# Loading K in one piece and scoring it by key head, in a one-token attention and MLP kernel

## Chip, cores and metric

The kernel runs on one core of a Trainium2 chip. The metric is the device time of one execution in microseconds (us). The kernel before takes 98.69 us, the median of three runs (98.69 to 98.81). All figures beside it come from one execution that the hardware profiler recorded.

## The reference

One token with 1024 features is normalised; the result `xn` goes through an attention block and an MLP block, and both are added to the input.

```python
def _A_ref(x, k_cache, v_cache, wq, wo):
    B, Sq, D = x.shape                                 # 1, 1, 1024
    Hq, Dh = 32, 128
    Hkv, Sk = k_cache.shape[1], k_cache.shape[2]       # 4 key heads, 65536 keys
    W = min(4096, max(256, Sk // 4))                   # the last 4096 keys
    rep = Hq // Hkv                                    # 8 query heads share a key head
    q = (x @ wq).reshape(B, Sq, Hq, Dh) ...
    k = jnp.repeat(k_cache[:, :, Sk - W:, :], rep, axis=1)
    v = jnp.repeat(v_cache[:, :, Sk - W:, :], rep, axis=1)
    scores = jnp.einsum("bhqd,bhkd->bhqk", q, k) * (Dh ** -0.5)
    p = _softmax(scores, axis=-1)
    o = jnp.einsum("bhqk,bhkd->bhqd", p, v)
    return (...).reshape(B, Sq, Hq * Dh) @ wo

def _B_ref(x, w1, b1, w2, b2):                         # F = 3584
    y = _layernorm(x, axis=-1)
    h = _gelu(jnp.einsum("bsd,df->bsf", y, w1) + b1)
    return jnp.einsum("bsf,fd->bsd", h, w2) + b2

xn = _layernorm(x, axis=-1)
return x + _A_ref(xn, ...) + _B_ref(xn, ...)
```

All weights and caches are bf16. Per execution the kernel reads wq (8.4 MB), the last 4096 keys of K for four heads (4.2 MB), W1 (7.3 MB), the same of V (4.2 MB), W2 (7.3 MB) and wo (8.4 MB), each once.

## The kernel before

The kernel is written out by hand: every engine has its own list of instructions, and semaphores tie the lists together. There is no scheduler; the order in the text is the order on each engine.

**SP's queue** issues all large loads, in this order: wq in two pieces, K in two pieces (`load_k(0)`, `load_k(1)`, L228 and L229), W1, and then, each behind a wait, V (L303, after the last transpose of K, since V is written over K in `KV`), W2 in two pieces (L305, after the last scores, since W2 is written over wq in `BIG`), and wo in four pieces (L308, after the hidden layer, over W1). The transfers go through one queue in that order.

**K.** `load_k(c)` brings two of the four key heads at a time. Their 4096 keys are cut into 64 runs; a partition of `KV` gets one run of one head, 64 keys of 128 features or 16 KB, so the 128 partitions are 64 runs times two heads. VectorE then transposes `KV` into `KT` in four pieces (`turn_k`, L277, four transposes of 128 x 4096 bf16, handled as 2048 words of 32 bits), in blocks of 32 partitions by 32 words. After that the partitions of `KT` carry features and its columns carry keys: neighbouring words of a row belong to alternating heads, and the two halves of a word are two neighbouring features.

**Queries.** TensorE multiplies the normalised token with wq into bank 7 (L427, eight turns of eight matmuls), ScalarE copies the result out (`Q32`, L286), VectorE transposes it (`QTB`, L288), and VectorE and ScalarE place it into `QBD`, which is zero elsewhere, in four copies (L299, L301).

**Scores.** `OTHER` and `ALT` are constants made by GpSimd at the start. Four matmuls (L434) write −1e30 into those places of banks 3 to 6 where a query head would meet the keys of the other head of the pair, and zero elsewhere; each is followed by two matmuls on zeros (`busy`) that keep TensorE running. Then 32 matmuls of 512 columns (L452 to L461) add the scores: over two pairs, two halves, two banks, two halves of a word (`w`) and two halves of the features (`j`). The moving operand is `K4`, and with it neighbouring columns of a matmul are neighbouring words of `KT`, 4 bytes apart:

```python
K4 = KT[:, :].rearrange("p (x k w) -> p x w k", k=64, w=2)
...
K4[:, bass.ds(c * 64 + i * 32 + 16 * n, 16), w, 32 * j:32 * j + 32]
```

**Softmax.** VectorE takes the maximum over the four banks in two pieces (L324), gathers the quarters of the partitions (L328, L330) and writes the negative scaled maximum, with −1e30 in the rows of the other pair (`MASKC`), into `NMB` (L333). ScalarE takes exp of all 2048 columns twice (L338), once for each pair, with row sums into `SUMP`; it writes each pair's two of four neighbouring columns of `P`. VectorE transposes `P` into `PT` (L343).

**The rest, in TensorE's order.** After the scores TensorE waits for W1 (L467) and computes the hidden layer (seven turns of eight matmuls); it then adds the row sums (L474), turns the hidden layer into columns (L477), multiplies `PT` with V (L483, eight turns of four matmuls, needs `PT` and V), and runs eleven rounds of eight matmuls (L489) over the 28 row blocks of W2 and the first 16 of wo. Each round waits on `s_feed`, which GpSimd raises as W2 and wo land. The last 16 row blocks of wo go through narrow matmuls (L504), and the result is copied out and stored.

Of the kernel before, what the change touches and what calls it, by code (L numbers as in the profile page):

```python
# [5 lines left out]
ALU = mybir.AluOpType  # L6
ACTF = mybir.ActivationFunctionType
AX = mybir.AxisListType
# [6 lines left out]
REP = HQ // HKV  # L15
SK = 65536
W = 4096
# [10 lines left out]
PAIRS = 2  # L28
FAR = -1e30
QW = 512 + 32  # L30
# [24 lines left out]
def bass_parallel_sum__sliding_block_cached__mixer_channel_mlp__decode_kernel(  # L55
# [13 lines left out]
    SCALE = float(DH) ** -0.5  # L69
# [15 lines left out]
    DVE = Track(nc, "S_DVE")  # L85
    ACT = Track(nc, "S_ACT")
    POOL = Track(nc, "S_POOL")
# [14 lines left out]
    MASKC = sb("MASKC", [32, PAIRS], f32)  # L102
    OTHER = sb("OTHER", [2, 128], bf16)
    ALT = sb("ALT", [2, 512], bf16)
# [4 lines left out]
    BN = sb("BN", [128, 24], f32)  # L109
# [6 lines left out]
    QBD = sb("QBD", [128, PAIRS * QW], bf16)  # L116
# [5 lines left out]
    NMB = sb("NMB", [128, PAIRS], f32)  # L122
# [5 lines left out]
    SUMP = sb("SUMP", [128, PAIRS], f32)  # L128
    TOT = sb("TOT", [128, 1], f32)
# [9 lines left out]
    P, PT = KT[:, 0:4096], KT[:, 4096:8192]  # L139
# [16 lines left out]
    C = {}  # L156
# [14 lines left out]
    def pool_wait():  # L171
# [5 lines left out]
    C["QBD"] = POOL.mark(pool.memset(QBD[:, :], 0.0))  # L177
# [9 lines left out]
    POOL.mark(pool.memset(OTHER[:, :], FAR))  # L187
    POOL.mark(pool.memset(ALT[:, :], 0.0))
# [12 lines left out]
    POOL.mark(pool.affine_select(  # L201
        out=OTHER[:, :].rearrange("p (x g h) -> p x g h", g=2, h=REP),
        in_=OTHER[:, :].rearrange("p (x g h) -> p x g h", g=2, h=REP),
        pattern=[[0, 8], [-1, 2], [0, REP]], compare_op=ALU.not_equal, fill=0.0, base=0, channel_multiplier=1))
    POOL.mark(pool.affine_select(
        out=ALT[:, :].rearrange("p (x g) -> p x g", g=2), in_=ALT[:, :].rearrange("p (x g) -> p x g", g=2),
        pattern=[[0, 256], [-1, 2]], compare_op=ALU.not_equal, fill=1.0, base=0, channel_multiplier=1))
    for c in range(PAIRS):
        POOL.mark(pool.affine_select(  # L209
            out=MASKC[:, c:c + 1], in_=YZ[0:32, 0:1], pattern=[[0, 1]], compare_op=ALU.is_ge, fill=FAR,  # L210
            base=-16 if c else 15, channel_multiplier=1 if c else -1))
# [9 lines left out]
    def pairs(cache, c):  # L221
        return cache[0, 2 * c:2 * c + 2, SK - W:SK, :].rearrange("g (m i) d -> m g (i d)", m=64)
# [54 lines left out]
    def turn_k(n):  # L277
        dve.wait_ge(s_k[n // 2], 16)
# [13 lines left out]
    QD = QBD[:, :].rearrange("p (c x) -> p c x", c=PAIRS)[:, :, 0:512].rearrange("p c (w n e) -> p w c n e", w=2, e=2)  # L292
    QS = QTB.rearrange("p (j e c w) -> p w c j e", j=4, e=2, w=2)
    for b in range(4):
        rows = slice(32 * b, 32 * b + 32)
        to = QD[rows, :, :, 32 * b:32 * b + 16, :].rearrange("p w c (u j) e -> p w c u j e", j=4)
        of = QS[rows, :, 0:4 * PAIRS, :, :].rearrange("p w (c u) j e -> p w c u j e", c=PAIRS)
# [5 lines left out]
    sp.dma_start(V, A_v_cache[0, :, SK - W:SK, :].rearrange("g (m i) d -> m g (i d)", m=32)).then_inc(s_v, 16)  # L303
    sp.wait_ge(done["sc"], 4)
# [16 lines left out]
    S = PS[:, 3 * 512:7 * 512]  # L321
    for n in range(2):
        dve.wait_ge(done["sc"], 3 + n)
        C["mx"] = DVE.mark(dve.tensor_reduce(  # L324
            out=MX2[:, n:n + 1], in_=S[:, 1024 * n:1024 * n + 1024], axis=AX.X, op=ALU.max))
# [6 lines left out]
    for b in range(4):  # L332
        C["nmb"] = DVE.mark(dve.scalar_tensor_tensor(  # L333
            out=NMB[32 * b:32 * b + 32, :], in0=MXR[:, :].to_broadcast([32, PAIRS]), scalar=-SCALE, in1=MASKC[:, :],
            op0=ALU.mult, op1=ALU.add))
    act.wait_ge(DVE.sem, C["nmb"])
    for c in range(PAIRS):
# [30 lines left out]
    DVE.mark(dve.tensor_reduce(  # L368
        out=TOT[:, :], in_=PS[:, 3 * 512:3 * 512 + PAIRS], axis=AX.X, op=ALU.add))
    dve_wait()  # L370
    DVE.mark(dve.reciprocal(out=REC[:, :], in_=TOT[:, :]))
    dve_wait()
# [43 lines left out]
    def add(to, lhsT, rhs, **place):  # L416
        return pe.matmul(to, lhsT=lhsT, rhs=rhs, start=False, stop=False, skip_group_check=True, **place)  # L417
# [15 lines left out]
    with pe.Fori(0, 4) as n:  # L433
        pe.matmul(PS[:, bass.ds(n * 512 + 3 * 512, 512)], lhsT=OTHER[:, :], rhs=ALT[:, :], start=True, stop=False,  # L434
                  skip_group_check=True)
        busy(GO, bank(1), start=False, stop=False)
# [13 lines left out]
    pe.wait_ge(DVE.sem, C["d_QBD"])  # L450
# [23 lines left out]
    pe.matmul(PS[:, 3 * 512:3 * 512 + PAIRS], lhsT=B128[:, :], rhs=SUMP[:, :]).then_inc(done["tot"], 1)  # L474
# [77 lines left out]
```

## Time and profile before

| What | Value |
|---|---|
| Median of three runs | 98.69 us (98.69 to 98.81) |
| The profiled execution | 98.65 us |
| Its span in the profile | 97.2 us |
| Bytes moved | 39.88 MB, mean 410 GB/s over the span |
| TensorE busy, matmuls | 80.1 us (82% of the span), 389 matmuls |
| VectorE, ScalarE, GpSimd busy | 33.3, 13.0 and 9.7 us |
| Granted TensorE clock | full in every slice |

The span is the time between the first and last instruction that the profiler saw; the device time holds some 1.4 us more. A busy share is an average over the whole span and says little about which wait ends last. What decides is the chain of waits, which is followed back from the last instruction, and the idle time in front of each group on its engine with what ended it. Times "from the start" below count from the start of the span. PE stands for TensorE, PEld for its weight loads, DVE for VectorE, ACT for ScalarE, POOL for GpSimd, SP for SyncE; a "q" behind a name means its sequencer or its issuing of transfers.

The stretches between the landings of the loads look like this (start and end in us, busy time of TensorE's matmuls, share of DMA, rate):

| Stretch | Landing at its end | TensorE busy | DMA share | GB/s |
|---|---|---|---|---|
| 22.40 to 32.20 | K | 9.63 | 1.13 | 479 |
| 32.20 to 49.10 | W1 | 15.47 | 0.95 | 411 |
| 49.10 to 58.80 | V | 9.29 | 1.00 | 432 |
| 58.80 to 75.80 | W2 | 15.74 | 1.00 | 432 |
| 75.80 to 95.20 | wo | 17.43 | 0.95 | 406 |

A packet counts in the stretch in which it begins, which is why a share can pass 1 and its neighbour stay under it.

### The profile page before, as it was taken

The numbers are of one execution on the slowest core, as the hardware profiler recorded it, in microseconds if no ns is written. First come the engines' busy times: TensorE is split into PE (matmuls) and PEld (weight loads), VectorE is DVE, ScalarE is ACT, GpSimd is POOL, SyncE is SP. The second block draws the span as 40 slices with busy tenths as digits, with TensorE's granted clock in tenths as the row PEclk, the third lists the DMA queues.
The fourth block names the chain that finished last, engine by engine and source line by source line (L and its number), as shares of the span: only waits on it lengthen the run. The fifth ranks groups of instructions, "written<-read, shape, count | busy, mean of one in ns | idle before, by whom it ended". The sixth has DMA issues, their size and how long they took to land.

```text
span 97.2 us, 1407 instructions
## 1 busy us (share of the span) xinstructions
PE 80.1 (82%) x389; PEld 33.8 (35%) x400; DVE 33.3 (34%) x54; ACT 13.0 (13%) x20; POOL 9.7 (10%) x25
## 2 busy tenths in 40 slices
PE   0000999997999999999669999799999999779982
PEld 0000233443444432344134444433343443334451
DVE  0000589860069995000760593050049100000001
ACT  0880000050000005000019400200000100000001
POOL 6999300000000000000000000000000000000000
PEclk9999999999999999999999999999999999999999
DMA  2998888899999988888999999999899999889890
GB/s 64 650 473 377 377 377 377 377 452 425 414 418 516 637 377 377 377 377 377 499 431 445 431 431 445 431 431 394 374 485 485 445 445 445 381 374 445 377 384 2
DMA packets 1845, 39.88 MB, mean 410 GB/s; under 512 B 306, under 2 KB 308, under 8 KB 564
## 3 DMA queue, kind: packets, MB, share of 16 engines
q1 hardware_dynamic: 1732, 39.85, 95.6%
q10 hardware_dynamic: 112, 0.01, 0.1%
q8 instruction: 1, 0.02, 0.1%
HBM read 39.86 MB, written 0.00 MB: 410 GB/s over the span
## 4 chain that ended last, share of the span: by engine, by line
DMA 80%; PE 14%; SPq 3%; issue 1%; DVE 0%
DMA BIG<-in_B_w_dram 47%; DMA BIG<-in_A_wo_dram 33%; PE PS L417 14%; SPq L225 1%; SPq L160 1%; SPq L310 1%; DVE Pb L395 0%; PE PS L499 0%
## 5 line engine op out<-in xcount | busy, mean ns | idle before, releaser
L417 PE MATMUL PS<-BIG,GO 128*128 (+1 forms) x137 | 21.5, 334 | 2.2 <-POOLq L408 1.2
L417 PEld LDWEIGHTS PS<-BIG,GO 128*128 (+1 forms) x148 | 9.9, 97 | 13.9 <-issue 5.9
L417 PE MATMUL PS<-BIG,XZ 128*128 x64 | 14.0, 379 | 0.6 <-DMA BIG<-in_A_wq_dram 0.6
L417 PE MATMUL PS<-BIG,YZ 128*128 x56 | 12.4, 379 | 1.8 <-DMA BIG<-in_B_w_dram 1.8
L279 DVE STREAM_TRANSPOSE KT<-KV 128x2048 f32<-128x2048 f32 x4 | 9.0, 2290 | 6.8 <-DMA KV<-in_A_k_cache_dram 6.8
L421 PE MATMUL PS<-QBD 128*128 128x512 bf16 x38 | 11.2, 467 | 0.1
L417 PEld LDWEIGHTS PS<-BIG,XZ 128*128 x64 | 6.2, 98 | 8.3 <-issue 2.0
L413 PE MATMUL PS<-XBRP,onesb 1*128 1x512 bf16 x2 | 1.0, 605 | 9.7 <-DMA XBRP<-in_A_x_dram 9.7
L417 PE MATMUL PS<-KV,KT 128*128 x32 | 8.3, 381 | 0.5
L417 PEld LDWEIGHTS PS<-BIG,YZ 128*128 x56 | 5.4, 96 | 8.9 <-issue 3.0
L395 DVE CAST Pb<-PS 64x256 bf16<-64x256 f32 x1 | 0.4, 417 | 19.9 <-PE PS L499 19.9
L417 PE MATMUL PS<-KT,QBD 128*128 x32 | 7.1, 378 | 0.0
L421 PEld LDWEIGHTS PS<-QBD 128*128 128x128 bf16 x38 | 4.3, 115 | 7.4 <-issue 4.8
L343 DVE STREAM_TRANSPOSE KT<-KT 128x4096 bf16<-128x4096 bf16 x1 | 4.4, 4446 | 4.1 <-ACT KT L338 4.1
L338 ACT ACTIVATE KT<-PS,NMB 128x2048 bf16<-128x2048 f32 x2 | 3.9, 1963 | 12.1 <-DVE NMB L333 12.1
L324 DVE TENSOR_REDUCE MX<-PS 128x1 f32<-128x1024 f32 x2 | 2.5, 1225 | 8.2 <-PE PS L417 8.2
L237 DVE BATCH_NORM_STATS2 BN<-PS 128x6 f32<-128x512 f32 x2 | 1.3, 689 | 10.7 <-PE PS L413 10.7
L417 PEld LDWEIGHTS PS<-KV,KT 128*128 x32 | 3.1, 96 | 5.3 <-issue 3.8
L417 PEld LDWEIGHTS PS<-KT,QBD 128*128 x32 | 3.0, 97 | 4.0 <-issue 0.4
L375 DVE TENSOR_SCALAR QBD<-PS,REC 32x128 f32<-32x128 f32 x4 | 1.4, 345 | 6.9 <-PE PS L417 6.8
L413 PEld LDWEIGHTS PS<-XBRP,onesb 1*128 1x128 bf16 x2 | 0.1, 98 | 9.6 <-POOL MASKC L209 9.6
L395 ACT ACTIVATE Pb<-PS 64x256 bf16<-64x256 f32 x1 | 0.4, 381 | 19.5 <-PE PS L499 19.5
(78 smaller groups left out, 42.0 us busy)
## 6 DMA issues: line engine op xcount, KB each, us to landing
BIG<-in_A_wq_dram SPq DMA_DIRECT2D x1, 7168.0 KB, 21.1
BIG<-in_B_w_dram SPq DMA_DIRECT2D x1, 7168.0 KB, 46.1
KV<-in_A_k_cache_dram SPq DMA_DIRECT2D x2, 2048.0 KB, 27.8
KV<-in_A_v_cache_dram SPq DMA_DIRECT2D x1, 4096.0 KB, 22.1
BIG<-in_B_w_dram SPq DMA_DIRECT2D x1, 4096.0 KB, 20.8
BIG<-in_A_wo_dram SPq DMA_DIRECT2D x1, 4096.0 KB, 23.5
BIG<-in_B_w_dram SPq DMA_DIRECT2D x1, 3072.0 KB, 27.7
BIG<-in_A_wo_dram SPq DMA_DIRECT2D x1, 3072.0 KB, 30.4
```

Of the source, the lines that this page charges most:

```text
L160: sp.dma_start(dst[:, c0 * width:(c0 + n) * width].rearrange("p (c n) -> p c n", c=n), src[:, c0:c0 + n, :],).then_inc(semaphores[j], 16)
L225: sp.dma_start(KV[:, c * 8192:(c + 1) * 8192], pairs(A_k_cache, c)).then_inc(s_k[c], 16)
L237: DVE.mark(dve.bn_stats(out=BN[:, 12 * n + 6 * i:12 * n + 6 * i + 6], in_=src[:, 512 * i:512 * i + 512]))
L279: C["kt", n] = DVE.mark(dve.transpose(KT[:, n * 4096:(n + 1) * 4096].bitcast(f32), KV[:, n * 4096:(n + 1) * 4096].bitcast(f32)))
L310: sp.dma_start(BIG[:, first:first + n * D], wo_flat[:, c0 * D:(c0 + n) * D]).then_inc(s_wo[j] if j else s_feed, HALF_FEED)
L324: C["mx"] = DVE.mark(dve.tensor_reduce(out=MX2[:, n:n + 1], in_=S[:, 1024 * n:1024 * n + 1024], axis=AX.X, op=ALU.max))
L338: C["exp"] = ACT.mark(act.activation(out=P.rearrange("p (r x g) -> p r x g", r=2, g=4)[:, :, :, 2 * c:2 * c + 2], in_=S.rearrange("p (x r ...
L343: C["d_pt"] = DVE.mark(dve.transpose(PT, P))
L375: DVE.mark(dve.tensor_scalar(out=ONM[:, 128 * j:128 * j + 128], in0=PS[32 * j:32 * j + 32, 512 + 128 * j:512 + 128 * j + 128], scalar1=REC ...
L413: last = pe.matmul(bank(2 + i), lhsT=onesb[0:1, :], rhs=XB[0:1, 8 * i:8 * i + 8, :])
L417: return pe.matmul(to, lhsT=lhsT, rhs=rhs, start=False, stop=False, skip_group_check=True, **place)
L421: pe.matmul(to, lhsT=zeros[:, 0:128], rhs=zeros[:, 0:512], skip_group_check=True, **how)
```

## The change

All four key heads of K come in one load, in the layout that V already has: 32 runs of 128 keys for each head, 32 KB per partition, the partitions being 32 runs times four heads. After the transposes the words of four heads alternate in `KT`, and the scores pick one head at a time: eight columns of a head lie four words, 16 bytes, apart. No head meets another head's keys, so nothing is masked, the scores fill two banks instead of four, and one exp over 1024 columns takes the place of two over 2048. `P` has to be zero where a row's head doesn't own the column, so VectorE multiplies the exp, repeated four times, with a table `OWN` of ones and zeros (128 x 4).

In the order of the engines: the masking matmuls become matmuls on zeros of the same size; the score loop runs over two halves and four heads with four matmuls to a turn; the third and fourth transpose of K come after the copies into `QBD`; V's load waits for the fourth, as before. The constants `OTHER`, `ALT` and `MASKC` are gone, `QBD` is about twice as wide and is cleared in two pieces. `BN` gets a wider allocation of which the same columns are used.

```diff
-    s_k = sems("s_k", PAIRS)
+    s_k = nc.alloc_semaphore("s_k")
...
+    OWN = sb("OWN", [128, GROUPS], bf16)
...
-    BN = sb("BN", [128, 24], f32)
+    BN = sb("BN", [128, 96], f32)
...
-    QBD = sb("QBD", [128, PAIRS * QW], bf16)
+    QBD = sb("QBD", [128, GROUPS * QW], bf16)
...
-    P, PT = KT[:, 0:4096], KT[:, 4096:8192]
+    P, PT, PX = KT[:, 0:4096], KT[:, 4096:8192], KT[:, 8192:9216]
...
-    C["QBD"] = POOL.mark(pool.memset(QBD[:, :], 0.0))
+    C["QBD"] = POOL.mark(pool.memset(QBD[:, 0:1024], 0.0))
...
-    POOL.mark(pool.memset(OTHER[:, :], FAR))
-    POOL.mark(pool.memset(ALT[:, :], 0.0))
+    POOL.mark(pool.memset(QBD[:, 1024:], 0.0))
...
-    def load_k(c):
-        sp.dma_start(KV[:, c * 8192:(c + 1) * 8192], pairs(A_k_cache, c)).then_inc(s_k[c], 16)
+    def by_group(cache):
+        return cache[0, :, SK - W:SK, :].rearrange("g (m i) d -> m g (i d)", m=32)
...
-    load_k(0)
-    load_k(1)
+    sp.dma_start(KV[:, :], by_group(A_k_cache)).then_inc(s_k, 16)
...
-    for n in range(4):
+        DVE.mark(dve.tensor_reduce(
+            out=OWN[:, :], in_=identb[:, :].rearrange("p (b g h) -> p g b h", b=4, g=GROUPS), axis=AX.XY, op=ALU.add))
+
+    dve.wait_ge(s_k, 16)
+    for n in range(2):
         turn_k(n)
...
             C["a_QBD"] = ACT.mark(act.activation(out=to, in_=of, func=ACTF.Copy))
+    for n in range(2, 4):
+        turn_k(n)
     sp.wait_ge(DVE.sem, C["kt", 3])
...
-    sp.wait_ge(done["sc"], 4)
+    sp.wait_ge(done["sc"], 2 * GROUPS)
...
-    S = PS[:, 3 * 512:7 * 512]
+    S = PS[:, 3 * 512:5 * 512]
...
-    for c in range(PAIRS):
-        C["exp"] = ACT.mark(act.activation(
-            out=P.rearrange("p (r x g) -> p r x g", r=2, g=4)[:, :, :, 2 * c:2 * c + 2],
-            in_=S.rearrange("p (x r g) -> p r x g", r=2, g=2),
-            func=ACTF.Exp, bias=NMB[:, c:c + 1], scale=SCALE, accum_out=SUMP[:, c:c + 1]))
+    C["exp"] = ACT.mark(act.activation(
+        out=PX, in_=S, func=ACTF.Exp, bias=NMB[:, :], scale=SCALE, accum_out=SUMP[:, :]))
     dve.wait_ge(ACT.sem, C["exp"])
+    DVE.mark(dve.tensor_tensor(
+        out=P.rearrange("p (x g) -> p x g", g=GROUPS), in0=PX.unsqueeze(2).to_broadcast([128, 1024, GROUPS]),
+        in1=OWN[:, :].unsqueeze(1).to_broadcast([128, 1024, GROUPS]), op=ALU.mult))
+    dve_wait()
     C["d_pt"] = DVE.mark(dve.transpose(PT, P))
...
-    K4 = KT[:, :].rearrange("p (x k w) -> p x w k", k=64, w=2)
-    with pe.Fori(0, PAIRS) as c:
+    pe.reg_mov(turn, C["d_QBD"])
+    K4 = KT[:, :].rearrange("p (x j k g w) -> p x j g w k", j=2, k=REP, g=GROUPS, w=2)
+    with pe.Fori(0, 2) as i:
         pe.wait_ge(ACT.sem, C["a_QBD"])
-        with pe.Fori(0, 2) as i:
-            for n in range(2):
-                for w in range(2):
-                    for j in range(2):
-                        last = add(PS[:, bass.ds(i * 1024 + (3 + n) * 512, 512)],
-                                   QBD[:, bass.ds(c * 512 + (w * 256 + j), 128, step=2)],
-                                   K4[:, bass.ds(c * 64 + i * 32 + 16 * n, 16), w, 32 * j:32 * j + 32])
+        pe.wait_ge(DVE.sem, turn)
+        pe.reg_add(turn, turn, C["kt", 3] - C["d_QBD"])
+        with pe.Fori(0, GROUPS) as g:
+            for w in range(2):
+                for j in range(2):
+                    last = add(PS[:, bass.ds(i * 512 + 3 * 512, 512)],
+                               QBD[:, bass.ds(g * 512 + (w * 256 + j), 128, step=2)],
+                               K4[:, bass.ds(i * 64, 64), j, bass.ds(g, 1), w, :])
             last.then_inc(done["sc"], 1)
```

More of the change, by code (lines that the diff above doesn't have):

```diff
@@ L27 @@
 XW = 136
-PAIRS = 2
-FAR = -1e30
-QW = 512 + 32
+GROUPS = 4
+QW = 512 + 16
 XP = 72
@@ L121, in bass_parallel_sum__sliding_block_cached__mixer_channel_mlp__decode_kernel @@
     MXR = sb("MXR", [32, 1], f32)
-    NMB = sb("NMB", [128, PAIRS], f32)
+    NMB = sb("NMB", [128, 1], f32)
     Pb = sb("Pb", [128, 2048], bf16)
@@ L127, in bass_parallel_sum__sliding_block_cached__mixer_channel_mlp__decode_kernel @@
     QTB = Pb[:, 512:1024]
-    SUMP = sb("SUMP", [128, PAIRS], f32)
-    TOT = sb("TOT", [128, 1], f32)
+    SUMP = sb("SUMP", [128, 1], f32)
     REC = sb("REC", [128, 1], f32)
@@ L277, in turn_k @@
     def turn_k(n):
-        dve.wait_ge(s_k[n // 2], 16)
         C["kt", n] = DVE.mark(dve.transpose(
             KT[:, n * 4096:(n + 1) * 4096].bitcast(f32), KV[:, n * 4096:(n + 1) * 4096].bitcast(f32)))
-    for n in range(4):
+    with nc.allow_low_precision(reason="sums of a one and zeros"):
+        DVE.mark(dve.tensor_reduce(
+            out=OWN[:, :], in_=identb[:, :].rearrange("p (b g h) -> p g b h", b=4, g=GROUPS), axis=AX.XY, op=ALU.add))
+    dve.wait_ge(s_k, 16)
+    for n in range(2):
         turn_k(n)
@@ L332, in bass_parallel_sum__sliding_block_cached__mixer_channel_mlp__decode_kernel @@
     for b in range(4):
[L333 to L335 removed]
+        C["nmb"] = DVE.mark(dve.tensor_scalar(
+            out=NMB[32 * b:32 * b + 32, :], in0=MXR[:, :], scalar1=-SCALE, scalar2=None, op0=ALU.mult))
     act.wait_ge(DVE.sem, C["nmb"])
[L337 to L341 removed]
+    C["exp"] = ACT.mark(act.activation(
+        out=PX, in_=S, func=ACTF.Exp, bias=NMB[:, :], scale=SCALE, accum_out=SUMP[:, :]))
     dve.wait_ge(ACT.sem, C["exp"])
+    DVE.mark(dve.tensor_tensor(
+        out=P.rearrange("p (x g) -> p x g", g=GROUPS), in0=PX.unsqueeze(2).to_broadcast([128, 1024, GROUPS]),
+        in1=OWN[:, :].unsqueeze(1).to_broadcast([128, 1024, GROUPS]), op=ALU.mult))
+    dve_wait()
     C["d_pt"] = DVE.mark(dve.transpose(PT, P))
@@ L367, in bass_parallel_sum__sliding_block_cached__mixer_channel_mlp__decode_kernel @@
     dve.wait_ge(done["tot"], 1)
[L368 to L371, printed above, removed]
+    DVE.mark(dve.reciprocal(out=REC[:, :], in_=PS[:, 3 * 512:3 * 512 + 1]))
     dve_wait()
@@ L433, in bass_parallel_sum__sliding_block_cached__mixer_channel_mlp__decode_kernel @@
     with pe.Fori(0, 4) as n:
-        pe.matmul(PS[:, bass.ds(n * 512 + 3 * 512, 512)], lhsT=OTHER[:, :], rhs=ALT[:, :], start=True, stop=False,
+        pe.matmul(PS[:, bass.ds(n * 512 + 3 * 512, 512)], lhsT=GO[:, 0:128], rhs=GO[:, 0:512], start=True, stop=False,
                   skip_group_check=True)
@@ L473, in bass_parallel_sum__sliding_block_cached__mixer_channel_mlp__decode_kernel @@
     pe.wait_ge(ACT.sem, C["exp"])
-    pe.matmul(PS[:, 3 * 512:3 * 512 + PAIRS], lhsT=B128[:, :], rhs=SUMP[:, :]).then_inc(done["tot"], 1)
+    pe.matmul(PS[:, 3 * 512:3 * 512 + 1], lhsT=B128[:, :], rhs=SUMP[:, :]).then_inc(done["tot"], 1)
     pe.wait_ge(ACT.sem, C["a_h8"])
```

28 lines of the change are left out of this document (6 added, 22 removed).

## The prediction

> **What bounds the kernel now.** I read the chain of waits first, then the DMA page, then the timeline of TensorE, then the groups by shape.
>
> ```profile
> DMA 80%; PE 14%; SPq 3%; issue 1%; DVE 0%
> ...
> q1 hardware_dynamic: 1732, 39.85, 95.6%
> ```
>
> Chain and queues: the end hangs on DMA, and SP's queue keeps all 16 engines 95.6% busy over the span. 39.85 MB pass through one queue in the order wq, K, K, W1, V, W2, W2, wo. Time goes only if fewer microseconds of transfer remain, and is lost if the queue runs dry or TensorE falls behind the last transfers. So the cover of TensorE is what has to be read:
>
> ```profile
> 36.75 0.54 SPq L303 DMA_DIRECT2D KV<-in_A_v_cache_dram  x1
> 47.70 0.83 SPq L160 DMA_DIRECT2D BIG<-in_B_w_dram  x2
> 61.98 1.76 SPq L310 DMA_DIRECT2D BIG<-in_A_wo_dram  x4
> ```
> ```profile
> 40.56 7.11 PE L417 MATMUL PS<-KT,QBD 128*128 x32
> 49.51 12.44 PE L417 MATMUL PS<-BIG,YZ 128*128 x56 [1.84 <-DMA BIG<-in_B_w_dram]
> ...
> 62.95 8.73 PE L417 MATMUL PS<-KV,KT 128*128 x32
> 71.77 12.79 PE L417 MATMUL PS<-BIG,GO 128*128 x49
> 85.75 8.56 PE L417 MATMUL PS<-BIG,GO 128*128 x68 [1.19 <-POOLq L408]
> 94.61 0.73 PE L417 MATMUL PS<-BIG,GO 128*32 128x256 bf16 x20 [0.31 <-DMA BIG<-in_A_wo_dram]
> ```
>
> First column is the start, second the length, in us. TensorE runs scores, hidden layer, P·V, W2 and wo rounds in one line, and waits for data three times from the scores on: 1.84 us before the hidden layer, 1.19 before the first wo round, 0.31 before the last rows. So the scores may end 1.84 us later for nothing, and the hidden layer may start 1.19 + 0.31 = 1.50 us later before the end moves. From 40.56 to 49.51 + 1.50 = 51.0 there are 10.45 us for 32 score matmuls: 0.326 us each, against (7.11 − 0.38) / 31 = 0.217 now.
>
> **K in one load.** Two loads of 16 KB rows take from wq's landing (1.26 + 21.1 = 22.4) to the transposes' release at 32.2: 9.8 us. V, the same bytes in 32 KB rows, takes from W1's landing (3.04 + 46.1 = 49.1) to its own (36.75 + 22.1 = 58.85): 9.7 us. Gain 0.1 us (0.05 to 0.2 by the rounding), and one issue of some 0.6 us less on SP at a time when nothing waits for SP.
>
> The first two transposes lose their early start (27.52): all K lands at 32.1. Two of them (4.5 us) end at 36.6, before the copy of q frees VectorE at 37.2, so that costs nothing. The other two now stand behind the q transpose and the QBD copies (0.45 + 0.57, ending at 38.3) and end at 42.8. The second half of the scores needs them at 40.56 + 3.5 = 44.0 at the earliest: hidden by the first half. V's issue moves from 36.75 to 42.8; W1 covers it until 49.1.
>
> **Set-up.** POOL loses five constants (0.2 + 0.5 + 0.4 + 2.3 + 0.3) and gains about 1.0 for the other half of QBD; TensorE starts with x at 9.67 anyway. VectorE gains the reduction for OWN, at most the 1.03 us of the 128x512 reduction at L272, in its 6.6 us of idling for K. QBD copies have as many elements as before, the zeroing matmuls as many columns as the masking ones.
>
> **From scores to P.** The last maximum starts at 47.70 and exp at 50.64: 2.9 us, less 0.55 for half the columns (1225 ns for 1024) = 2.4. One exp of 1024 columns: half of 1963 plus 0.2 for its sum, 1.2 to 1.3, for two (3.9 + 0.4). New is the spread, 4096 elements on VectorE between exp and transpose. The nearest row, L256, multiplies 1024 bf16 by a repeated operand in 1225 ns: four times that is 4.9 us; the transpose of 4096 bf16 takes 4.45. I take 4.5. With the transpose: 2.4 + 1.25 + 4.5 + 4.45 = 12.6 us after the scores. P·V starts 12.44 + 1.0 after the hidden layer starts, so with the hidden layer right behind the scores the cover is 0.8 us, 0.4 at 4.9. Without cover each microsecond of it would delay P·V by one.
>
> **The scores.** Still 32 matmuls of 512 columns, now in eight turns of four. P·V has that form and takes 8.73 us, so 7.1 to 8.7 by the rows: at 8.7 they end at 49.3, inside the 1.84.
>
> The open price is the read of K. Before, a matmul reads columns 4 bytes apart (one bf16 of each pair); now the eight of a head lie 16 bytes apart, each column a piece by itself. No row of TensorE reads that. Lower end: no price, 0.217. The rows that bound it:
>
> ```profile
> L260 DVE TENSOR_REDUCE XNT<-Pb 128x8 f32<-128x1024 bf16 x1 | 2.0, 1986 | 0.0
> L324 DVE TENSOR_REDUCE MX<-PS 128x1 f32<-128x1024 f32 x2 | 2.5, 1225 | 8.2 <-PE PS L417 8.2
> L417 PEld LDWEIGHTS PS<-FLIP,H 8*128 8x128 bf16 x4 | 0.2, 113 | 0.6 <-ACT H L345 0.6
> L440 PEld LDWEIGHTS PS<-B1R,E 32*128 32x128 bf16 x4 | 0.2, 92 | 0.4 <-issue 0.4
> ```
>
> After the bar: busy us, mean ns of one. L260 sums 1024 bf16 read 16 bytes apart, exactly the new step: 1986 ns, where a reduction over as many adjacent elements takes 1225. With some 150 ns fixed (a reduction of 8 elements, L330, takes 149) that is 1.79 ns an element against 1.05. TensorE's weight load of H8 in steps of 8 bytes takes 113 ns, one of adjacent columns 92: a step costs there too, though only 0.16 ns a column. TensorE's own bound: the W1 matmuls read pieces of four columns (8 bytes) 56 bytes apart at full rate, 0.423 ns a column, so a separate piece costs it no more than 4 × 0.423 = 1.69 ns. With one column to a piece that is at most 512 × 1.69 = 866 ns a matmul.
>
> The ends are far apart: 0.217 us (hidden; by the weight loads' 0.16 ns, 0.30, hidden too) and 0.866. I take 0.866: L260 reads with this very step, at 1.79 ns, and a fetch of about 1.7 ns for each piece fits the reduction, and leaves W1 at full rate as the trace has it.
>
> [...]
>
> **Sum.** 32 × 0.866 = 27.7: the scores end at 68.3, the hidden layer starts there, 18.8 us later than 49.51; P (68.3 + 12.6 = 80.9) is ready before P·V (62.95 + 18.8 = 81.7). The waits of 1.19 and 0.31 vanish: the end moves by 18.8 − 1.5 = 17.3. The profiled execution took 98.65 (span 97.2, 1.4 around it), 0.04 under the median of 98.69: 98.65 + 17.3 = 115.9.
>
> Behind SP's wait for the scores stand W2's two loads and then wo. W2 is issued at 68.7 instead of 47.70; V is through at 58.7, and the first issue of the run (0.80) shows transfers about 1 us later, so DMA stands still for some 11 us. All of wo is in at 95.2 + 11 = 106, TensorE's last round is later (85.75 + 18.8 − 1.2 = 103.3 for its start, and 10 more), so TensorE sets the end.
>
> **Rivals.**
> - *Half rate.* 0.433 us a matmul: scores end at 54.4, the hidden layer 4.9 late, end +3.4: **102.1**. W2 is issued at 54.8, in time before V's end. For it: a step costs VectorE a factor of 1.7, not 4; TensorE may fetch a piece in less than the 1.69 that its rows allow. Against: VectorE's 1.79 ns for one piece.
> - *The step costs TensorE nothing that shows* (not slower). Place: the K read. Price up to 0.326 us a matmul. The scores stay under the loads of W1 and V, and the 0.1 us of K remains: 98.65 − 0.1 = **98.55**. It holds as long as 32 scores end by 51.0, and tips beyond. For it: full rate at 4 bytes and at W1's pieces, weight loads that lose only a fifth. Against: L260. If the one load gains nothing either, 98.65.
> - *The spread is late.* At L260's 1.79 ns it would take 7.3 us, 2.8 over, 2 us past its cover; TensorE's 1.5 us of waits take most: **99.2**, with free scores. Against: L256 repeats an operand in the same way at 1.2 ns.
>
> **Chances.** Full price per piece 0.43 (own range 112.5 to 117.5: a piece at 1.5 to 1.79 ns), half rate 0.22, hidden 0.30, spread late 0.05. A difference of 0.2% (0.2 us) is about what a measurement of this kernel can tell from none. Of the hidden case 0.10 falls beyond that as faster, 0.17 inside, 0.03 slower; all else is slower: 0.10, 0.17, 0.73. The range must hold the hidden case and the full price to reach 8 in 10: 98.4 to 117.
>
> **What would show it.** The 32 scores in the timeline: 27 us (forecast), 14 (half), 7 to 10 (hidden); starts 0.87, 0.43 or 0.22 to 0.3 apart. W2's issue near 68.7, and a hole in DMA of 11 us from 58.7. The wait of 1.19 for wo gone, or, if hidden, still 0.5 or more. K in 9.7 us. Spread 4.4 to 4.9, exp near 1.1. The forecast falls if the scores run at under 0.33 us each.

## The result and the profile after

The changed kernel takes 116.38 us, the median of six runs (115.58 to 116.89), where the kernel before took 98.75 beside it (98.62 to 99.16): a ratio of 1.1775, 95% interval 1.1727 to 1.1823. The profiled execution took 116.37 us, its span is 114.9. The forecast was 115.9. The ratios in this document leave out executions that ran more than 1.5% above the fastest of the same kernel.

First the page of the kernel after: the granted clock and the rate of the DMA engines in 40 slices of 2.87 us, the large queue, the chain.

```profile
PEclk9999999999999996555555556999999999999999
...
GB/s 114 571 320 639 319 319 639 285 446 368 585 419 319 639 319 319 502 365 491 422 0 0 0 137 399 377 388 442 419 508 434 365 525 374 454 357 299 0 6 1
...
q1 hardware_dynamic: 1588, 39.85, 81.4%
...
PE 78%; DMA 18%; issue 1%; ACT 1%; DVE 0%; SPq 0%
```

The chain was 80% DMA and is now 78% TensorE. The same 39.85 MB pass, but the queue is busy for 81.4% of the span, not 95.6%: three slices in the middle move nothing. What holds TensorE is the first line of its timeline from the scores on; the lines after it follow without a wait for a load:

```profile
39.64 27.63 PE L400 MATMUL PS<-KT,QBD 128*128 x32
67.09 14.31 PE L400 MATMUL PS<-BIG,YZ 128*128 x56
...
82.40 8.73 PE L400 MATMUL PS<-KV,KT 128*128 x32
```

The scores take 27.63 us instead of 7.11. Behind them the hidden layer starts at 67.09 instead of 49.51 (+17.6); it also takes 14.31 instead of 12.44, so P·V starts 19.45 later. The waits for W1 and wo are gone, and from the start of the W2 rounds to the last narrow matmul TensorE takes 21.80 instead of 23.57: 19.45 − 1.77 = 17.7, the whole loss. K was in 9.7 us after wq, as forecast. SP's issues and VectorE's part show the rest of the stage:

```profile
42.74 0.55 SPq L289 DMA_DIRECT2D KV<-in_A_v_cache_dram  x1
67.29 0.81 SPq L156 DMA_DIRECT2D BIG<-in_B_w_dram  x2
```
```profile
32.03 4.50 DVE L258 STREAM_TRANSPOSE KT<-KV 128x2048 f32<-128x2048 f32 x2 [10.83 <-DMA KV<-in_A_k_cache_dram]
...
38.21 4.50 DVE L258 STREAM_TRANSPOSE KT<-KV 128x2048 f32<-128x2048 f32 x2
...
70.91 4.43 DVE L325 TENSOR_TENSOR KT<-KT,OWN 128x4096 bf16<-128x4096 bf16 x1 [1.27 <-ACT KT L322]
75.37 4.45 DVE L329 STREAM_TRANSPOSE KT<-KT 128x4096 bf16<-128x4096 bf16 x1
```

All keys are turned at 42.7, early enough for the second half of the scores. W2 is issued when the scores are done, at 67.29, long after V is in at 58.6, so DMA stands still for the 9.7 us until W2's first packets at 68.3. P is ready at 79.8, before P·V.

Why the scores are slow is in the starts of their weight loads, one for each matmul (timeline of TensorE's weight loads in the kernel after, the end of the scores and the beginning of the hidden layer):

```profile
64.51 0.12 PEld L400 LDWEIGHTS PS<-KT,QBD 128*128 x1 [0.74 <-issue]
65.37 0.13 PEld L400 LDWEIGHTS PS<-KT,QBD 128*128 x1 [0.73 <-issue]
...
67.49 0.15 PEld L400 LDWEIGHTS PS<-BIG,YZ 128*128 x1 [0.28 <-issue]
67.92 0.15 PEld L400 LDWEIGHTS PS<-BIG,YZ 128*128 x1 [0.28 <-issue]
```

A score matmul starts every 0.858 us, 1.68 ns for each of its 512 columns. It does so from 39.64 to about 43.6 us at full granted clock and in the same way afterwards, when the granted clock has fallen to half:

```profile
22.40:32.03 9.63, 9.55 (x45) 4.43 (x46) 0.00 (x0) 0.00 (x0) 0.00 (x0) 1.00 1.11 477
32.03:48.90 16.87, 16.87 (x50) 4.54 (x49) 9.99 (x7) 1.43 (x3) 0.00 (x0) 0.84 0.95 412
48.90:58.60 9.70, 9.70 (x13) 1.46 (x12) 0.69 (x1) 0.00 (x0) 0.00 (x0) 0.50 0.88 378
58.60:67.30 8.70, 8.70 (x12) 1.27 (x11) 0.00 (x0) 0.00 (x0) 0.00 (x0) 0.50 0.00 0
```

These windows of the kernel after give TensorE's busy time, its weight loads, VectorE, ScalarE, GpSimd, and then the granted clock, the DMA share and GB/s. The first fifteen slices of the page, up to 43.1 us, are at full clock, and the 0.84 of the second window is half the clock for some 5.3 of its 16.87 us; so the clock fell at about 43.6 us, 4 us into the scores, and not at 46, as the first expectation below has it. Although TensorE counts as busy for 8.70 of 8.70 us, it is granted half the clock, and that lasts into the hidden layer, whose first nine matmuls start 0.427 us apart until 70.9, then 0.217 as before: 9 × 0.21 = 1.9 us, the difference of 14.31 and 12.44.

### The profile page after: what moved, and what is told of

Same layout as the page of the kernel before. It is cut to its first block, busy times and chain, and to the rows that moved or that the text cites. A ratio compares the mean times of both kernels' runs of the same rounds, so it can differ in the third digit from the quotient of the medians.

```text
span 114.9 us, 1424 instructions
## 1 busy us (share of the span) xinstructions
PE 101.6 (88%) x400; PEld 35.6 (31%) x400; DVE 36.6 (32%) x55; ACT 10.2 (9%) x18; POOL 7.0 (6%) x20
## 3 DMA queue, kind: packets, MB, share of 16 engines
q1 hardware_dynamic: 1588, 39.85, 81.4%
## 4 chain that ended last, share of the span: by engine, by line
PE 78%; DMA 18%; issue 1%; ACT 1%; DVE 0%; SPq 0%
PE PS L400 75%; DMA BIG<-in_A_wq_dram 18%; PE PS L404 2%; PE PS L417 1%; ACT H L331 1%; PE PS L431 0%; DVE Pb L378 0%; SPq L156 0%; PE PS L423 0%; PE PS L483 0%
## 5 line engine op out<-in xcount | busy, mean ns | idle before, releaser
L400 PE MATMUL PS<-KT,QBD 128*128 x32 | 27.6, 1036 | 0.0
L400 PE MATMUL PS<-BIG,YZ 128*128 x56 | 14.3, 419 | 0.0
L400 PEld LDWEIGHTS PS<-BIG,GO 128*128 (+1 forms) x148 | 10.1, 97 | 12.0 <-issue 5.0
L258 DVE STREAM_TRANSPOSE KT<-KV 128x2048 f32<-128x2048 f32 x4 | 9.0, 2290 | 10.9 <-DMA KV<-in_A_k_cache_dram 10.8
L400 PEld LDWEIGHTS PS<-KT,QBD 128*128 x32 | 3.8, 122 | 22.5 <-issue 22.5
L310 DVE TENSOR_REDUCE MX<-PS 128x1 f32<-128x512 f32 x2 | 1.4, 692 | 23.9 <-PE PS L400 23.9
L400 PEld LDWEIGHTS PS<-BIG,YZ 128*128 x56 | 5.9, 105 | 9.5 <-issue 4.0
L325 DVE TENSOR_TENSOR KT<-KT,OWN 128x4096 bf16<-128x4096 bf16 x1 | 4.4, 4426 | 1.3 <-ACT KT L322 1.3
L217 DVE BATCH_NORM_STATS2 BN<-PS 128x6 f32<-128x512 f32 x2 | 1.3, 690 | 10.8 <-PE PS L396 10.8
L322 ACT ACTIVATE KT<-PS,NMB 128x1024 bf16<-128x1024 f32 x1 | 1.1, 1114 | 31.2 <-DVE NMB L319 31.2
```

What stands on the lines that cost most here:

```text
L217: DVE.mark(dve.bn_stats(out=BN[:, 12 * n + 6 * i:12 * n + 6 * i + 6], in_=src[:, 512 * i:512 * i + 512]))
L258: C["kt", n] = DVE.mark(dve.transpose(KT[:, n * 4096:(n + 1) * 4096].bitcast(f32), KV[:, n * 4096:(n + 1) * 4096].bitcast(f32)))
L310: C["mx"] = DVE.mark(dve.tensor_reduce(out=MX2[:, n:n + 1], in_=S[:, 512 * n:512 * n + 512], axis=AX.X, op=ALU.max))
L322: C["exp"] = ACT.mark(act.activation(out=PX, in_=S, func=ACTF.Exp, bias=NMB[:, :], scale=SCALE, accum_out=SUMP[:, :]))
L325: DVE.mark(dve.tensor_tensor(out=P.rearrange("p (x g) -> p x g", g=GROUPS), in0=PX.unsqueeze(2).to_broadcast([128, 1024, GROUPS]), in1=OWN ...
```

## The experiments

The question of the first four is what TensorE pays for: each separate column, or each stretch of 16 bytes that it has to touch. They change only from which words of `KT` the score loop takes a head's columns; the loads, loops and counts are those of the kernel after, so in these four a head's queries meet keys of other heads too, and only the times matter. Each of the four ran once. All edits below are against the kernel after unless another is named.

**Adjacent words (4 bytes).**

```diff
-    K4 = KT[:, :].rearrange("p (x j k g w) -> p x j g w k", j=2, k=REP, g=GROUPS, w=2)
+    K4 = KT[:, :].rearrange("p (x j g k w) -> p x j g w k", j=2, k=REP, g=GROUPS, w=2)
```

> The kernel after, except that the eight columns of a turn are eight neighbouring words of KT, 4 bytes apart, instead of every fourth word; so each head's queries meet keys of other heads too. Theory of the step (the price is the 16 bytes between one column and the next): a score matmul falls from 0.86 us to between 0.22 and 0.33, the 32 take 7 to 10.5 us, the granted clock stays full, and the time is 98.4 to 98.8 us. Rival (the price is the loop of eight turns of four matmuls, or TensorE's clock, which the profile after shows at half from 46 us on): the matmuls stay near 0.86 us and the time near 116.

Measured 99.93 us; the kernel before took 99.05 beside this and the next three. From the timeline of TensorE:

```profile
41.71 1.91 PE L400 MATMUL PS<-KT,QBD 128*128 x8
43.89 1.03 PE L400 MATMUL PS<-KT,QBD 128*128 x4 [0.27 <-issue]
45.22 1.02 PE L400 MATMUL PS<-KT,QBD 128*128 x4 [0.30 <-issue]
47.16 1.03 PE L400 MATMUL PS<-KT,QBD 128*128 x4 [0.92 <-DVE MX L310]
...
52.48 12.44 PE L400 MATMUL PS<-BIG,YZ 128*128 x56 [0.35 <-issue]
```

Within a turn the matmuls start 0.217 apart: the price is gone, and with it all but 0.9 us of the loss. The 98.4 to 98.8 expected were missed, for two reasons. Turns of four matmuls leave gaps of some 0.3 us, 0.9 at the change of halves, so the 32 end 10.4 us after the first start (52.1), and not the 7.1 to 8.7 that the prediction allowed for. And in this run they start 2 us late: TensorE waited 2.0 us for wq, the granted clock was at half from 24.2 to 27.6 us, and the query's matmuls took 15.7 us instead of 14.0.

**Every second word (8 bytes).**

```diff
-    K4 = KT[:, :].rearrange("p (x j k g w) -> p x j g w k", j=2, k=REP, g=GROUPS, w=2)
+    K4 = KT[:, :].rearrange("p (x j y w) -> p x j y w", j=2, y=32, w=2)
...
-                               K4[:, bass.ds(i * 64, 64), j, bass.ds(g, 1), w, :])
+                               K4[:, bass.ds(i * 64, 64), j, bass.ds(g, REP, step=2), w])
```

> The kernel after with the columns of a turn 8 bytes apart (every second word), so each head's queries meet keys of other heads too. By stretch (a price of 1.68 ns for each new stretch of 16 bytes, columns in the same stretch come with it): two columns share one, 0.43 us a matmul, scores 13.8 us, the end some 2 to 3 us later than before: 101 to 102. By piece (each column that doesn't touch its neighbour pays 1.68 ns): 0.86 us, 116. By bytes passed (16 bytes take 1.68 ns): 0.43 us, 101 to 102.

Measured 103.25. Starts of the weight loads, one for each matmul, at the change from head 3 of the first half of the keys to head 0 of the second:

```profile
46.52 0.12 PEld L400 LDWEIGHTS PS<-KT,QBD 128*128 x1 [0.46 <-issue]
47.09 0.12 PEld L400 LDWEIGHTS PS<-KT,QBD 128*128 x1 [0.46 <-issue]
47.67 0.13 PEld L400 LDWEIGHTS PS<-KT,QBD 128*128 x1 [0.45 <-issue]
48.10 0.12 PEld L400 LDWEIGHTS PS<-KT,QBD 128*128 x1 [0.31 <-issue]
48.53 0.12 PEld L400 LDWEIGHTS PS<-KT,QBD 128*128 x1 [0.31 <-issue]
```

The starts are 0.43 apart for heads 0 and 1, and 0.573 for heads 2 and 3. Here eight columns span 60 bytes: heads 0 and 1 begin on word 0 or 1, and their columns lie in four stretches of 16 bytes; heads 2 and 3 begin on word 2 or 3, and theirs lie in five. 0.43 / (64 × 4) = 1.68 ns a stretch, 0.573 / (64 × 5) = 1.79. So it is the stretch that is paid, not the column; by the column it would have been 0.86 again. The expectation of 101 to 102 had two columns in every stretch and overlooked the fifth one of heads 2 and 3, 16 matmuls at 0.14 us more. Of these 0.14 the fifth stretch at 1.68 ns makes 0.11; the rest, the 7% between 1.68 and 1.79, comes again in the next run. Adjacent words put eight columns in two stretches: 128 of them at 1.68 ns are 0.215 us, just the full rate.

**Every eighth word (32 bytes).**

```diff
-    K4 = KT[:, :].rearrange("p (x j k g w) -> p x j g w k", j=2, k=REP, g=GROUPS, w=2)
+    K4 = KT[:, :].rearrange("p (x y w) -> p x y w", y=64, w=2)
...
-                               K4[:, bass.ds(i * 64, 64), j, bass.ds(g, 1), w, :])
+                               K4[:, bass.ds(i * 64, 64), bass.ds(g + 4 * j, REP, step=8), w])
```

> The kernel after with the columns of a turn 32 bytes apart (every eighth word), so each head's queries meet keys of other heads too. By stretch and by piece: 0.86 us a matmul as at 16 bytes, 116 us. By bytes passed: 1.72 us a matmul, scores 55 us, some 144 us.

Measured 119.07; starts 0.918 apart, again 1.79 ns a stretch. Twice the distance costs 7% more and not twice as much, so the bytes passed over aren't what is paid. What the 7% are stays open.

**Two neighbours, then a step of 32 bytes.**

```diff
-    K4 = KT[:, :].rearrange("p (x j k g w) -> p x j g w k", j=2, k=REP, g=GROUPS, w=2)
+    K4 = KT[:, :].rearrange("p (x j q s e w) -> p x j s w q e", j=2, q=4, s=GROUPS, e=2, w=2)
...
-                               K4[:, bass.ds(i * 64, 64), j, bass.ds(g, 1), w, :])
+                               K4[:, bass.ds(i * 64, 64), j, bass.ds(g, 1), w, :, :])
```

> The kernel after with the columns of a turn in twos: two neighbouring words (8 bytes), then a step of 32 bytes; each head's queries meet keys of other heads too. By stretch and by piece: one fetch for two columns, 0.43 us a matmul, 101 to 102 us. By bytes passed (16 bytes per column on average): 0.86 us, 116 us. With the 8-byte step it tells stretch from piece: 0.43 in both is the stretch, 0.86 there and 0.43 here is the piece.

Measured 100.84. From the timeline of TensorE:

```profile
39.78 14.00 PE L400 MATMUL PS<-KT,QBD 128*128 x32
53.61 12.45 PE L400 MATMUL PS<-BIG,YZ 128*128 x56
```

The starts are 0.432 apart: two columns to a stretch, half the price of one, although the two are followed by a jump. At this pace the gaps between turns don't show, and the granted clock stays full (1.00 from 39 to 70 us).

**The loop.** The step of 16 bytes kept, in four turns of eight matmuls instead of eight of four.

```diff
-        with pe.Fori(0, GROUPS) as g:
-            for w in range(2):
...
+        with pe.Fori(0, GROUPS // 2) as h:
+            for g in range(2):
+                for w in range(2):
...
```

The indices of the operands and the counts that VectorE and SP wait for change with the loop.

> The kernel after with the score loop in four turns of eight matmuls instead of eight turns of four, the step still 16 bytes. Theory of the step: nothing changes, 0.859 us a matmul, 116 us, since a turn of four takes 3.4 us at this price and TensorE's queue hides the turn's own instructions. Rival (turns of four cost): the matmuls come closer together and the time falls by a microsecond or more.

Measured 116.25 in one run, starts still 0.858 apart (the kernel before beside this and the next three: 98.88, median of 17). The loop is no part of the price.

**The order written by VectorE.** The layout keeps K's one load; VectorE's transposes write a head's eight keys side by side, so that TensorE reads 4 bytes apart.

```diff
-            KT[:, n * 4096:(n + 1) * 4096].bitcast(f32), KV[:, n * 4096:(n + 1) * 4096].bitcast(f32)))
+            KT[:, n * 4096:(n + 1) * 4096].bitcast(f32).rearrange("p (x g k) -> p x k g", g=GROUPS, k=REP),
+            KV[:, n * 4096:(n + 1) * 4096].bitcast(f32)))
...
-    K4 = KT[:, :].rearrange("p (x j k g w) -> p x j g w k", j=2, k=REP, g=GROUPS, w=2)
+    K4 = KT[:, :].rearrange("p (x j g k w) -> p x j g w k", j=2, k=REP, g=GROUPS, w=2)
```

> The kernel after, except that VectorE's four transposes of K write each block of 32 words in the order of heads (head, key) instead of (key, head), so that the eight columns of a head are neighbouring words and the scores read them 4 bytes apart. The reads of K are as in the 4-byte look: 0.32 us a matmul by the turns of four, scores 10.3 us. The price moves to the writes of VectorE, which no row shows: between nothing (2.29 us a transpose as now) and one write of 1.79 ns for each word as the strided reduction reads (3.8 us). At nothing the scores run from 39.6 to 50 and the time is 98.5 to 98.9, the hidden case of the prediction. At 3.8 us the q transpose slips to 39.8, the fourth transpose ends at 48.5, V is issued there, just ahead of W1's end, and the scores end near 54: 101 to 102.

Measured 101.59, ratio 1.0263 (1.0229 to 1.0298), as the dear end of the expectation has it. Timeline of VectorE:

```profile
32.26 7.43 DVE L258 STREAM_TRANSPOSE KT<-KV 128x2048 f32<-128x2048 f32 x2 [10.82 <-DMA KV<-in_A_k_cache_dram]
39.54 0.40 DVE L273 STREAM_TRANSPOSE Pb<-Pb 128x256 f32<-128x256 f32 x1
...
40.57 7.43 DVE L258 STREAM_TRANSPOSE KT<-KV 128x2048 f32<-128x2048 f32 x2
```

The price has moved to VectorE. A transpose that writes 32 bytes apart takes 3.79 us (the mean of four) instead of 2.29; the query's transpose slips from 37.1 to 39.5, the fourth of K ends at 48.0, TensorE waits 1.6 and 2.3 us, and the hidden layer starts at 54.1.

**The same in turns of eight**, by the edit of the loop shown above.

> The kernel with the heads put in order by the transposes, and the score loop in four turns of eight matmuls. If the gap of 0.45 us between turns of four in the 4-byte look is the turn's own instructions, the matmuls come 0.22 us apart, the scores take 7 us and the time is 0.1 to 0.2 us under the kernel before (98.5 to 98.6 where that takes 98.7), if the transposes' writes cost nothing. Where they cost, the fourth transpose sets the scores' end and the loop saves at most 2 us of the other run's time.

Six executions took 100.37 to 106.69, with a median of 102.08; why three of them took over 102.5 is open. The ratio is 1.0209 (1.0141 to 1.0277): slower than the kernel before, but by how much is unclear. The profiled run took 100.37, with the hidden layer at 53.0 and TensorE waiting 1.9 us for the fourth transpose.

**The same, in turns of eight, with K in two loads of 16 KB a partition.**

```diff
-    sp.dma_start(KV[:, :], by_group(A_k_cache)).then_inc(s_k, 16)
+    for c in range(2):
+        sp.dma_start(KV[:, c * 8192:(c + 1) * 8192], by_group(A_k_cache)[:, :, c * 8192:(c + 1) * 8192]).then_inc(s_k[c], 16)
...
-    dve.wait_ge(s_k, 16)
+    dve.wait_ge(s_k[0], 16)
     for n in range(2):
         turn_k(n)
+    dve.wait_ge(s_k[1], 16)
```

> As the run with four turns of eight, but K in two loads of 16 KB per partition (the two halves of each run), so that only the one load of 32 KB is undone. By the trace of before, two loads cost 0.05 to 0.2 us more of transfer than one, and the first two transposes can start 4.7 us sooner, which nothing waits for if writes are cheap: 0.1 us slower than the one load. If the transposes are dear, the earlier start helps: faster by up to 2 us.

Measured 99.2, ratio 1.0005 (0.998 to 1.003): level with the kernel before. The first two transposes start at 27.71, and the query's is no longer late. So with this order two loads are what gives VectorE room. In the profiled execution, 99.38, TensorE still waits 3.2 us for the second half, the granted clock is at half from 47.4 to 50.8 us, and the hidden layer starts at 51.8. The 0.1 us that one load was to save is within the scatter: from wq's landing to K's it is 9.7 to 10.1 us in the eleven profiles with one load and 9.7 to 9.9 in the three with two.

**Mixed.** One load; the first half of K in pairs (TensorE pays 0.43), the second with all eight together. Against the turns of eight:

```diff
-        C["kt", n] = DVE.mark(dve.transpose(
-            KT[:, n * 4096:(n + 1) * 4096].bitcast(f32).rearrange("p (x g k) -> p x k g", g=GROUPS, k=REP),
-            KV[:, n * 4096:(n + 1) * 4096].bitcast(f32)))
+        words = KT[:, n * 4096:(n + 1) * 4096].bitcast(f32)
+        to = (words.rearrange("p (x q s e) -> p x q e s", q=4, s=GROUPS, e=2) if n < 2 else
+              words.rearrange("p (x g k) -> p x k g", g=GROUPS, k=REP))
+        C["kt", n] = DVE.mark(dve.transpose(to, KV[:, n * 4096:(n + 1) * 4096].bitcast(f32)))
...
-    K4 = KT[:, :].rearrange("p (x j g k w) -> p x j g w k", j=2, k=REP, g=GROUPS, w=2)
-    with pe.Fori(0, 2) as i:
+    K2 = KT[:, 0:8192].rearrange("p (x j q s e w) -> p x j s w q e", j=2, q=4, s=GROUPS, e=2, w=2)
+    K8 = KT[:, 8192:].rearrange("p (x j g k w) -> p x j g w k", j=2, k=REP, g=GROUPS, w=2)
+    for i, ready, K4 in ((0, C["d_QBD"], K2), (1, C["kt", 3], K8)):
...
```

> The one load of 32 KB kept. VectorE writes the first half of K so that two keys of a head are neighbours (a write step of 8 bytes), the second half so that all eight are. The first half is then read two columns to 16 bytes, the second 4 bytes apart, in turns of eight matmuls. By the stretch theory the first sixteen scores start 0.43 us apart and the last sixteen 0.217: 39.7 + 6.9 + 3.5 = 50.1 us, under the limit of 51.0, if the second half's transposes (3.7 us each, as in the order run) end by 46.6. What is open is the price of a write step of 8 bytes on VectorE. If it is nothing (2.3 us a transpose), all K is turned by about 45.7 and the time is 98.4 to 98.9, no slower than before. If it costs as the step of 32 bytes did (3.7), the query's transpose slips by 2 us, the scores end near 52 and the time is 99.2 to 100.2.

Measured 100.14, ratio 1.0154 (1.0105 to 1.0203). Each step of the sum up to the hidden layer came out, and the time didn't. The pairs cost VectorE nothing (two transposes in 4.50 us), all keys were turned at 45.7, and the timeline of TensorE has the scores where they should be:

```profile
39.71 10.55 PE L402 MATMUL PS<-KT,QBD 128*128 x32
50.10 12.43 PE L402 MATMUL PS<-BIG,YZ 128*128 x56
...
87.11 8.66 PE L402 MATMUL PS<-BIG,GO 128*128 x72 [1.25 <-POOLq L393]
```

But wo is late: the round that waits for it starts at 87.11 instead of 85.75. Of the 16 DMA engines 15 had brought the first 4 MB of wo by 85.4 us, as before, and one at 86.9. The queues of DMA within 77.60 to 78.80 us, with packets, MB and share, show what stood in its way:

```profile
q1 hardware_dynamic: 15, 0.49, 97.5%
q8 instruction: 1, 0.02, 4.9%
```

This is a fetch of 16 KB of instructions, 0.94 us on one engine, between pieces of wo. The 15 pieces of wo that begin in this window took 18.7 us together, 0.5 more than at the 1.21 of a piece that the other 15 between 77 and 79 us show; 0.94 and 0.5 are the lag of 1.4. Each program here has one such fetch within its span. In the kernel before it starts at 94.7, when the last of wo is under way, and that is in at 95.2 on all engines.

**The length of TensorE's program.** The mixed kernel with a shorter program, and the kernel before with a longer one and no other edit. `H8` is ScalarE's copy of the hidden layer, which four matmuls turn into columns.

```diff
-    for i, ready, K4 in ((0, C["d_QBD"], K2), (1, C["kt", 3], K8)):
+    for i, ready, K4, per in ((0, C["d_QBD"], K2, 1), (1, C["kt", 3], K8, 2)):
...
-        with pe.Fori(0, GROUPS // 2) as h:
-            for g in range(2):
+        with pe.Fori(0, GROUPS // per) as h:
+            for g in range(per):
...
-    for c in range(4):
-        last = add(turned[:, c], H8[:, c:512:4], FLIP[:, 0:7])
+    with pe.Fori(0, 4) as c:
+        last = add(turned[:, bass.ds(c, 1), :], H8[:, bass.ds(c, 128, step=4)], FLIP[:, 0:7])
...
```

The operands' indices and the counts that are waited for follow, and the wait for V comes ahead of the loop on H8.

> In the mixed run fifteen of sixteen DMA engines brought the first 4 MB of wo by 85.4 us, as before, and one at 86.9: on that engine a fetch of 16 KB of instructions stood between the pieces of wo from 77.74 to 78.68 us. In every other run the one such fetch comes some 3 us ahead of the end of the span, when all of wo is on its way or in. The mixed run had TensorE's loop over the two halves of the scores written out, 8 matmuls and their 8 weight loads more. Here TensorE's program is cut again: the first half of the scores in turns of four, and the four matmuls on H8 in a loop. If the fetch was TensorE's, and its place in the program decides when it falls, it is back behind 92 us, wo is in by 95.3 and the time is 98.4 to 98.9, level with before or 0.2 under it. If the late engine had another cause, it is late again and the time stays at 100.0.

And the kernel before, written out:

```diff
-        with pe.Fori(0, 2) as i:
+        for i in range(2):
             for n in range(2):
```

> The kernel before, with nothing but TensorE's inner loop over two halves of the scores written out (8 matmuls and their weight loads more in the program, the same 32 executed). If the length of TensorE's program decides where the fetch of instructions falls, it comes up to 17 us earlier, one DMA engine brings the first of wo some 1.4 us late and the time is 99.8 to 100.2. If the length has no part in it, the time is 98.5 to 98.9, as before.

The written-out kernel before takes 100.01, ratio 1.0122 (1.0102 to 1.0143), without any change to what is computed or moved. Its fetch starts at 80.3 us, and the first 4 MB of wo lands 25.0 us after its issue, where the kernel before has 23.5. Timeline of TensorE, beside the 85.75 and 1.19 of the kernel before:

```profile
87.30 8.58 PE L417 MATMUL PS<-BIG,GO 128*128 x72 [2.31 <-POOLq L408]
```

So the length of TensorE's program moves the fetch: it came at 77.7 and 80.3 us in the two programs whose text has 16 score matmuls, and in the last 4 us of the span in the twelve with 4 to 12.

The short program has its fetch back at 95.3, but takes 99.91, ratio 1.0123 (1.0103 to 1.0144). The loop on H8 was a mistake: one matmul to a turn, they start 0.6 us apart, and P·V starts at 65.88 instead of 63.53. V was late, too, 14.4 us from its issue at 45.7 and in at 60.0, but P·V came later than that here.

**Mixed, short, without the loop on H8**, and with three zeroing turns of four. Against the short program:

```diff
-    with pe.Fori(0, 4) as n:
+    with pe.Fori(0, 3) as n:
...
-    pe.wait_ge(s_v, 16)
-    with pe.Fori(0, 4) as c:
-        last = add(turned[:, bass.ds(c, 1), :], H8[:, bass.ds(c, 128, step=4)], FLIP[:, 0:7])
+    for c in range(4):
+        last = add(turned[:, c], H8[:, c:512:4], FLIP[:, 0:7])
+        if c == 0:
+            pe.wait_ge(s_v, 16)
```

> The mixed layout with TensorE's program as short as in the short run (the first half of the scores in turns of four), but with the four matmuls on H8 in a row again, and with three of the four zeroing turns (bank 6 holds no scores here). Scores from about 39.1, the second half's keys turned at 45.7, scores' end at 49.3, hidden layer at 49.5 as in the kernel before. If the two losses named in the mixed and the short run (the fetch of instructions at 77.7, the loop on H8) were all that kept this version back, wo is in by 95.2 and the time is 98.4 to 98.8, level with before; if V, issued at 45.7, comes too late for the end of W1, as it seemed in the short run (V in at 60.0 instead of 58.7), it is 99.2 to 99.8.

Measured 99.52 (98.85 to 101.46), ratio 1.004 (1.0008 to 1.0073). The scores run from 38.97 to 49.8, the fetch is at 94.8. What is left is V: issued at 45.66, 3.6 us before W1 is in, it landed at 59.9 in the profiled run, 14.3 us after its issue, and not at 58.8, and what stands behind it on the queue is 1.1 late. In the mixed run V was issued as late (45.75) and came at 58.7, 13.0 after, so this varies from run to run; its cause stays open. No version here beats the kernel before.

## Why the prediction was right

The mechanism was right step by step: TensorE's read of K costs what was forecast, the scores end long after W1 is in, W2's issue and all that follows move with them, and the waits at the end vanish. The range, 98.4 to 117, held all rivals and so tests little; what came out is the 115.9 and its steps. Two errors in the sum that nearly cancel are luck.

- *The read of K.* 0.866 us a matmul was forecast from one column to a piece and 1.69 ns a piece; 0.858 and 1.68 were measured. The upper bound from W1's matmuls (8-byte pieces at full rate) was the price itself, and L260 pointed to the right end. No row of TensorE told that the price lies at the bound; it was taken over from VectorE, with a chance of 0.43, and whether the two engines' prices have one cause isn't shown. The piece was called a separate column; the 8-byte and paired runs show that it is a stretch of 16 bytes, however many columns are read in it. W1's pieces, 8 bytes long and at multiples of 8, lie in one stretch each, 128 to a matmul, which at 1.68 ns is 0.215 us: so four columns to a stretch come at the full rate of 0.217 us, which is why they showed no price and why the bound worked out from them was exact. At 16 bytes column and stretch are the same; at other steps they aren't. For the half rate of the first rival stood only VectorE's factor of 1.7, and no run shows it at this step: one column to a stretch is a quarter of full rate, 0.858 against 0.217, and two are a half, 0.43.
- *The start of the scores*, taken as unchanged, is 0.92 us earlier (39.64 for 40.56). The zeroing matmuls were costed by columns. Before, a turn of them started every 0.855 us, now every 0.645. Their weights now come from 128 rows where those of `OTHER` had two; that this is the cause wasn't tried.
- *The hidden layer*, forecast 18.8 us late, is 17.6 late: 0.9 for the earlier start, 0.3 for 0.858 instead of 0.866.
- *The clock.* The half clock behind the slow scores wasn't in the sum: +1.9 us in the hidden layer. It and the earlier start with the faster read, 1.2 us the other way, nearly cancel, which is why the sum came within 0.5 of the median. That is luck: with the clock left out and the rest as measured the sum would have been 114.5.
- *The waits.* 1.5 us were to vanish; the stretch from the W2 rounds to the last rows got 1.77 shorter.
- *The stage behind.* Spread 4.43 (4.5 forecast), exp 1.11, V's issue 42.74 (42.8), P ready 2.6 us ahead of P·V (0.8 forecast; the slow clock added 1.9 of cover), the hole in DMA 9.7 (11, since W2 was issued at 67.29 and not 68.7), wo in at 106.1 (106) and not what sets the end.
- *The rivals.* The hidden case, 98.55, let the scores take up to 8.7 us from P·V's form. With a free read the same loop takes 10.4, and the hidden layer starts 10.8 after the first score (52.48 after 41.71, the run with adjacent words). From 39.64 that would be 50.4, inside the limit of 51.0 by 0.6, where 8.7 leaves 2.6: the turn of four when nothing slows the matmuls was mis-sized. The run itself started its scores 2 us later, ended past the limit and lost 0.9, so the case would have held only narrowly. The late spread fell: 4.43 us. Half rate is what pairs of columns give: 100.84 was measured with them where 102.1 was worked out, since the hidden layer started at 53.6 and not 54.4, from the earlier start, and the rest is within what one run tells.

## What to carry to other kernels

When a layout moves from one engine's convenience to another's, cost the moving operand's read in stretches of 16 bytes: with fewer than four bf16 columns in a stretch TensorE slowed down in proportion here (0.217 us a matmul with four, 0.432 with two, 0.858 with one), so the time follows from counting stretches before anything is built. A strided write on the engine that makes the layout need not be free either: a step of 32 bytes cost VectorE two thirds more (3.79 us for 2.29), and pairs cost it nothing (two transposes in 4.50) but TensorE twice the time (0.432 for 0.217). And in a kernel bound by DMA a longer unrolled loop can cost 1% (1.0122 here) by moving a fetch of instructions into the transfers, so look for the instruction queue in the trace before explaining such a loss by anything else.

## What the runs showed of the hardware

- TensorE read its moving operand, 512 columns of bf16, at 1.68 ns for each stretch of 16 bytes: 0.217 us with four columns to a stretch, 0.432 with two, 0.858 with one, the last at full and at half granted clock alike. With a step of 32 bytes (0.918 us), or five stretches to eight columns (0.573), it was 1.79, and why is open.
- The granted clock fell to half under matmuls that followed each other without a gap but read slowly: at 0.858 us a matmul from 43.6 us on, 4 us after the first, until 3.9 us after the hidden layer began (70.96 for 67.09). At 0.573 it did so once for 3.4 us (46.9 to 50.3 in the 8-byte run, 0.81 granted between 46 and 55 us), behind the first stretch of such matmuls and not behind the second, and at 0.432 not at all. What sets the clock isn't shown: from 48.9 to 67.3 us the profile calls TensorE busy for the whole time, and the granted clock is 0.50.
- VectorE's transposes of 2048 words took 2.29 us, no more with successive results 8 bytes apart (two in 4.50), and 3.79 with 32 bytes.
- A fetch of 16 KB of instructions held one DMA engine for 0.94 us in the mixed run and in the kernel before written out, and the wo that came behind it was 1.4 to 1.5 us late (86.9 us for 85.4; 25.0 us from its issue for 23.5).
